# Attention and gated MLP on one core: two weight guards moved to VectorE, and new planned times for the first units

## The chip, the cores and the metric

The kernel runs on one core of a Trainium2 chip. The metric is the time of one execution on the device in microseconds (us); lower is better. Three executions of the kernel before took 531.34 to 532.36 us, median 532.01 us. The profile shown below was taken from one execution of 531.34 us, whose span, from the first to the last instruction, is 529.6 us.

## The reference

Inputs are q, k, v of shape (8, 8, 576, 64) in float32, and three weights in float64 (`w_in` 512 x 1024, `conv_w` 3 x 1024, `w_out` 1024 x 512).

```python
scores = q @ k.T / sqrt(64)                      # per batch and head
mask = (rel >= 0) & (rel < 64)                   # rel = query position - key position
attn = softmax(where(mask, scores, -1e9))        # sum + 1e-9 in the divisor
x = (attn @ v) as (batch, seq, 512)
h = relu(x @ w_in)
conv = three-tap convolution of h over seq, per channel, with conv_w
out = (h * sigmoid(conv)) @ w_out
```

## The kernel before

**Units.** The 8 x 576 = 4608 sequence positions are cut into twelve units (u = 0 to 11) of 384. For every unit the work has two halves. The attention half forms banded scores on TensorE in three blocks b (`qk`, L340), takes row maxima on VectorE (`row_max`, L353), exponentials on ScalarE (`exps`, L362), a guarded reciprocal and the division (`guard`, `reciprocal`, `normalise`, L369 to L378), a transposition (units 0 and 1: on TensorE, with a copy back by `untile` on ScalarE, L387) and four products with v (`values`, c = 0 to 3, L477). Their result is split into a high part by ScalarE (`split_hi`, L485, tile `xh`) and a remainder by VectorE (`split_lo`, L488, tile `xl`). The second half is the MLP: for each of eight chunks f, `mm1` (L501, twelve matmuls into one of two `acc` banks), `relu` (L522), then per pair of chunks i the convolution (`conv_mid` on ScalarE, `conv_side` on VectorE, L535), sigmoid, gate (L547), its split (`gate_hi`, `gate_lo`, L555), and `mm2` (L564, twelve matmuls per chunk into four `po` banks). All matmuls of the MLP work on such split pairs, three products for one.

**The banks.** The `acc` banks 0 and 1 are taken in turn by the products with v and the chunks of `mm1`. Unit 0's c = 0 to 3 take 0, 1, 0, 1, and the chunks f = 0 and 1 then 0 and 1, so `mm1` of f = 0 can't start before `split_lo` of c = 2 has read bank 0.

**The weights.** They arrive as 64-bit words and are turned into float32 on the core (`to_f32`, L244): ScalarE takes the absolute value of the high words (L248), GpSimd bounds it from below with TINY so that the exponent arithmetic can't wrap (L249, the "guard" of this document; the softmax has another one at L370), VectorE shifts and masks (L250), puts sign and exponent in (L252), ScalarE scales the low words (L255), and VectorE adds them (L256). Then GpSimd makes the high part (L269) and VectorE the remainder (L270). Chunks f = 0 and f = 1 of `w_in` are converted alone (512 elements per partition), called in0 and in1 here; then in23, in45, in67 and out01 to out67 in pairs (1024 elements). The words land in four half buffers, so that a later pair's load waits until an earlier conversion has read its half.

**The order.** Every piece of work is entered with a planned time t (the dictionary `START`, L140, and offsets to it), an engine, a cost and the tiles that it reads and writes. The pass `queued` (L61) then lays out each engine's order: it goes forward in time with the costs, and whenever an engine is free it takes, of the pieces that are ready, the one with the smallest t. The order that comes out is fixed; on the chip every engine's queue runs in it. [...] The pass also puts small matmuls on a tile of zeros (`spare`, L212) into TensorE's early gaps, up to 110 us of its own clock; they compute nothing that is used.

Of the kernel before, what the change touches and what calls it, by code (L numbers as in the profile page):

```python
# [8 lines left out]
F32 = mybir.dt.float32  # L9
# [3 lines left out]
ALU = mybir.AluOpType  # L13
# [20 lines left out]
TINY = 2.0 ** -15  # L34
# [26 lines left out]
def queued(works, fill=None):  # L61
# [30 lines left out]
    while left:  # L92
# [17 lines left out]
        if fill and e == "PE" and start < FILL_TO:  # L110
# [4 lines left out]
            if n > 0 and clean:  # L115
                order.append(Work(x.t, e, 0.0, fill(n, min(clean)[1]), [], [], None, 0, 0.0))
        turn = SWITCH[e] if e in SWITCH and (x.kind != state[e] if e == "PE" else x.kind and x.kind != state[e]) else 0.0
        if turn and e == "PE" and not x.kind:
            turn = LEAVE
        if e == "PE" or x.kind:  # L120
# [17 lines left out]


START = {  # L140
    "v0": -27.5,
    "pv0": -15.968,
    "conv": -37.437,
    "bits": ((-46.561, -47.419), (-44.383, -45.007)),
    "qk1": -43.011,
    "v1": -11.849,
    "qk2": -2.185,
    "qk0": (-91.154, -52.794, -48.024),
    "ex0": (-42.377, -37.771, -19.993),
    "sc1": (-20.012, -18.408, -14.041),  # L150
    "ex1": (-8.106, -4.046, -3.778),
    "mask": -0.529,
    "sig": ((3.087, 7.079, 8.764, 10.751), (3.178, 6.73, 5.945, 9.966), (4.046, 6.806, 8.285, 10.314)),
    "in": (-39.031, -37.38, -33.878, -12.682, -12.013),
    "out": (-11.963, -8.679, 1.926, 7.315),
# [3 lines left out]
}  # L159
SWITCH = {"PE": 0.14, "ACT": 1.28}  # L160
LEAVE = 0.24
PORT_CL = 0.5
WARM = 5.0
FILL, FILL_FROM, FILL_TO = 4.0, 2.0, 110.0

# [2 lines left out]
def attention_moe(ctx: ExitStack, tc: tile.TileContext, q, k, v, w_in, conv_w, w_out, out):  # L168
    nc = tc.nc
# [4 lines left out]
    def many(n, shape, dt, name, where=pool):  # L174
        return [where.tile(shape, dt, name=f"{name}{i}") for i in range(n)]
# [7 lines left out]
    mask = many(3, [P, P], F32, "mask")  # L183
# [13 lines left out]
    bits = [flat.bitcast(U32)[:, 4 * DM * i:4 * DM * (i + 1)].rearrange("p (e two) -> p e two", two=2) for i in range(2)]  # L197
# [20 lines left out]
    def at(t, eng, cost, do, r=(), w=(), kind=None, mb=0, port=0.0):  # L218

        plan.append(Work(t, eng, cost, do, list(r), list(w), kind, mb, port))  # L220

    def two(t, eng, cost, do, **kw):
        at(t, eng, cost, do, port=cost, **kw)
# [17 lines left out]

    def to_f32(t, n, st, x, kb, kt):  # L244

        lw, hw, xu = st[..., 0], st[..., 1], x.bitcast(U32)

        at(t, "ACT", 0.0009 * n + 0.2, lambda: nc.scalar.activation(x, hw.bitcast(F32), AF.Abs), r=kb, w=kt)  # L248
        at(t, "POOL", 0.0027 * n + 0.02, lambda: nc.gpsimd.tensor_scalar(x, x, TINY, None, op0=ALU.max), w=kt, port=PORT_CL)  # L249
        two(t, "DVE", 0.00052 * n + 0.06, lambda: nc.vector.tensor_scalar(  # L250
            xu, xu, 3, 0x3FFFFFF8, op0=ALU.logical_shift_left, op1=ALU.bitwise_and), w=kt)
        two(t, "DVE", 0.00104 * n + 0.07, lambda: nc.vector.scalar_tensor_tensor(  # L252
            xu, hw, 0xC0000000, xu, op0=ALU.bitwise_and, op1=ALU.bitwise_or), r=kb, w=kt)

        at(t, "ACT", 0.0009 * n + 0.2, lambda: nc.scalar.activation(lw, lw, AF.Copy, scale=2.0 ** -29), w=kb)  # L255
        two(t, "DVE", 0.00104 * n + 0.07, lambda: nc.vector.tensor_tensor(xu, xu, lw, ALU.add), r=kb, w=kt)  # L256

    def weights(t, src, fs, hi, lo, key, buf, halves):

        e = slice(halves[0] * DM, (halves[-1] + 1) * DM)  # L260
        st, x = bits[buf][:, e], w24[buf][:, e]
        kb, kt = [("bits", buf, a) for a in halves], [("w24", buf, a) for a in halves]
        for f, a, tl in zip(fs, halves, load_at(buf, halves, t)):
            at(tl, "SP", 0.7, lambda f=f, a=a: nc.sync.dma_start(
                bits[buf][:, a * DM:(a + 1) * DM], src[f].bitcast(U32).rearrange("p (e two) -> p e two", two=2)),
               w=[("bits", buf, a)], mb=0.52)
        n = len(fs) * DM
        to_f32(t, n, st, x, kb, kt)
        two(t, "POOL", 0.00127 * n, lambda: nc.gpsimd.tensor_copy(hi, x), r=kt, w=[f"{key}{f}h" for f in fs])  # L269
        two(t, "DVE", 0.00104 * n + 0.07, lambda: nc.vector.tensor_tensor(lo, x, hi.bitcast(F32), ALU.subtract),  # L270
           r=kt + [f"{key}{f}h" for f in fs], w=[f"{key}{f}l" for f in fs])

    freed = {}

    def load_at(buf, halves, t):

        ts = [freed.get((buf, a), START["bits"][buf][a]) for a in halves]
        for a in halves:
            freed[(buf, a)] = t + 0.01
        return ts  # L280

    def weights_in(t, fs, *where):
        f = slice(fs[0], fs[-1] + 1)
        weights(t, w_in, fs, wih[:, f].rearrange("p f c e -> p (f c e)"),
                wil[:, f].rearrange("p f c e -> p (f c e)"), "in", *where)

    def weights_out(t, fs, *where):
        f = slice(fs[0], fs[-1] + 1)
        weights(t, w_out, fs, woh[:, f].rearrange("p f e -> p (f e)"), wol[:, f].rearrange("p f e -> p (f e)"), "out", *where)

    def weights_conv(t_load, t):
        at(t_load, "SP", 0.7, lambda: nc.sync.dma_start(
            cbits, conv_w.bitcast(U32).rearrange("p (e two) -> p e two", two=2)), w=["cbits"], mb=0.03)
        to_f32(t, 3 * NF, cbits, cw.rearrange("p k f -> p (k f)"), ["cbits"], ["cw"])
# [436 lines left out]
```

## Time and profile before

| | |
|---|---|
| median of three executions | 532.01 us |
| the profiled execution | 531.34 us, span 529.6 us |
| TensorE (PE) busy | 518.5 us, 98% of the span |
| VectorE (DVE) busy | 380.3 us, 72% |
| ScalarE (ACT) busy | 379.7 us, 72% |
| GpSimd (POOL) busy | 112.6 us, 21% |
| granted TensorE clock | full over the whole span |

In rows of the profile the first column is a start or a stretch in us from the first instruction, and a busy time is the union of an engine's instructions in it. "L249" is a line of the kernel. A bracket at the end of a timeline row gives the idle time of the engine before the instruction, and what ended it. Matmuls overlap in the records: one 384-column matmul lasts 0.34 us in them, while the next starts about 0.18 us after it.

### The profile page before, as it was taken

Reading aid. Unit: us, or ns where it says so; the run is one execution under the profiler, and the core shown is the slowest. Engines: PE = TensorE matmul, PEld = TensorE weight load, DVE = VectorE, ACT = ScalarE, POOL = GpSimd, SP = SyncE. Lnnn points to the kernel's source line nnn. Section 1 sums busy time; section 2 is a strip of 40 time slices with the busy share of each in tenths; the row PEclk is TensorE's granted clock in tenths of the full one; section 3 lists DMA queues with packets and bytes.
Section 4 is the critical chain, followed back from the end, with each engine's and each line's share of the span. In section 5 each row is a group of like instructions: output and inputs, shape, how many; then the busy total and the mean of one; then the engine's idle time right before and its main releaser. Section 6 shows DMA issues by size and latency. Waiting matters only on the chain.

```text
span 529.6 us, 14836 instructions
## 1 busy us (share of the span) xinstructions
PE 518.5 (98%) x5826; PEld 499.8 (94%) x5826; DVE 380.3 (72%) x1084; ACT 379.7 (72%) x1011; POOL 112.6 (21%) x196
## 2 busy tenths in 40 slices
PE   9998999999999999999999999999999999999996
PEld 8887889999999999999999999999999999999996
DVE  3899999985858667767767767767767667655552
ACT  2997897579896696696697687687687687544542
POOL 6664467113131011021021021021021021000000
PEclk9999999999999999999999999999999999999999
DMA  8984660237292173183083074073073053010011
GB/s 284 365 296 136 208 231 1 60 109 248 76 325 72 58 256 83 42 291 77 21 297 77 16 253 122 21 285 105 13 264 120 17 152 104 16 61 0 2 60 62
DMA packets 29463, 69.98 MB, mean 132 GB/s; under 512 B 5713, under 2 KB 17617, under 8 KB 29393
## 3 DMA queue, kind: packets, MB, share of 16 engines
q1 hardware_dynamic: 29392, 69.03, 39.7%
q8 instruction: 46, 0.75, 0.6%
q14 instruction: 25, 0.20, 0.1%
HBM read 47.73 MB, written 9.47 MB: 108 GB/s over the span
## 4 chain that ended last, share of the span: by engine, by line
PE 85%; DVE 9%; DMA 1%; ACT 1%; issue 1%; SPq 1%; POOL 0%; DVEq 0%
PE po L564 39%; PE acc L501 36%; PE acc L481 6%; PE sc L350 5%; DVE c L535 1%; DVE w L252 1%; DMA T<-in_w_in_dram 1%; DVE s L357 1%; DVE w L256 1%; DVE wil L270 1%; ACT s L367 1%; SPq L234 1%; DVE xl L488 1%; DVE s L378 1%; DVE w L250 1%
## 5 line engine op out<-in xcount | busy, mean ns | idle before, releaser
L501 PE MATMUL acc<-xh,wih 128*128 128x384 f32 x384 | 131.5, 342 | 0.8 <-DVE xl L488 0.8
L564 PE MATMUL po<-gh,woh 128*128 128x386 f32 (+1 forms) x384 | 132.1, 344 | 0.0
L535 DVE SCALAR_TENSOR_TENSOR c<-hbuf,cw,c 128x386 f32<-128x386 f32 (+1 forms) x192 | 109.6, 623 | 30.7 <-ACT c L528 30.7
L564 PE MATMUL po<-gh,wol 128*128 128x386 f32 (+1 forms) x384 | 129.9, 338 | 0.0
L564 PE MATMUL po<-gl,woh 128*128 128x386 f32 (+1 forms) x384 | 129.7, 338 | 0.0
L501 PE MATMUL acc<-xh,wil 128*128 128x384 f32 x384 | 129.7, 338 | 0.0
L501 PE MATMUL acc<-xl,wih 128*128 128x384 f32 x384 | 129.7, 338 | 0.0
L367 ACT ACTIVATE s<-s,nm 128x96 f32<-128x96 f32 (+2 forms) x288 | 105.1, 367 | 5.2 <-DVE nm L357 4.9
L555 DVE TENSOR_TENSOR gl<-c,gh 128x772 fp32r<-128x772 f32 (+1 forms) x48 | 55.8, 1162 | 28.2 <-ACT gh L551 28.1
L501 PEld LDWEIGHTS acc<-xh,wih 128*128 128x128 f32 x384 | 72.1, 188 | 2.9 <-POOL sm L370 0.7
L564 PEld LDWEIGHTS po<-gh,woh 128*128 128x128 f32 x384 | 72.2, 188 | 2.6
L378 POOL TENSOR_TENSOR s<-s,r 128x768 f32<-128x768 f32 x27 | 39.7, 1472 | 163.5 <-DVE r L373 150.7
L547 DVE TENSOR_TENSOR c<-c,hbuf 128x772 f32<-128x772 f32 (+1 forms) x48 | 47.4, 987 | 36.9 <-ACT c L542 36.7
L564 PEld LDWEIGHTS po<-gl,woh 128*128 128x128 f32 x384 | 72.3, 188 | 0.0
L564 PEld LDWEIGHTS po<-gh,wol 128*128 128x128 f32 x384 | 72.3, 188 | 0.0
L501 PEld LDWEIGHTS acc<-xh,wil 128*128 128x128 f32 x384 | 72.2, 188 | 0.0
L501 PEld LDWEIGHTS acc<-xl,wih 128*128 128x128 f32 x384 | 72.1, 188 | 0.0
L522 ACT ACTIVATE hbuf<-acc 128x384 f32<-128x384 f32 x64 | 30.9, 486 | 45.8 <-PE acc L501 45.4
L542 ACT ACTIVATE c<-c 128x772 f32<-128x772 f32 (+1 forms) x48 | 40.7, 848 | 30.2 <-DVE c L535 29.9
L357 DVE CUSTOM_DVE_ANT_0 s<-sc,mask 128x96 f32<-128x96 f32 (+2 forms) x272 | 51.5, 254 | 9.7 <-POOL mask L321 5.7
L367 ACT ACTIVATION_READ_ACCUMULATOR s<-s,nm 128x1 f32 x288 | 54.3, 189 | 0.0
L511 POOL COPY hbuf<-hbuf 128x4 f32<-128x4 f32 x44 | 16.7, 379 | 176.3 <-DVE c L547 176.2
(64 smaller groups left out, 644.5 us busy)
## 6 DMA issues: line engine op xcount, KB each, us to landing
v<-in_v_dram SPq DMA_DIRECT2D x24, 768.0 KB, 7.2
ub<-T SPq DMA_DIRECT2D x240, 48.0 KB, 1.9
k<-in_k_dram SPq DMA_DIRECT2D x22, 448.0 KB, 4.9
q<-in_q_dram SPq DMA_DIRECT2D x22, 384.0 KB, 6.9
out_dram<-T SPq DMA_DIRECT2D x8, 772.0 KB, 4.2
T<-in_w_in_dram SPq DMA_DIRECT2D x8, 512.0 KB, 6.6
T<-in_w_out_dram SPq DMA_DIRECT2D x8, 512.0 KB, 4.2
out_dram<-T SPq DMA_DIRECT2D x3, 768.0 KB, 6.4
```

What stands on the lines that cost most here:

```text
L350: nc.tensor.matmul(banks_of(u, b)[h][r:r + rows, i * P + o:i * P + n], qs[hs, 2 * g + p, t:t + rows], ks[hs, 2 * g + p, t + o:t + n], star ...
L357: nc.vector.tensor_tensor_reduce(out=ss[b][:, i, h, o:n], in0=banks_of(u, b)[h][:, i * P + o:i * P + n], in1=mask[m][:, o:n], scale=-0.125 ...
L367: nc.scalar.activation(x, x, AF.Exp, bias=nms[b][:, e], scale=-1.0, accum_out=sms[b][:, e])
L378: on.tensor_tensor(sv, sv, rs[b].unsqueeze(2).broadcast_to([P, 2 * NB, n]), ALU.mult)
L481: nc.tensor.matmul(acc[bank(("v", u, c))][h * D:(h + 1) * D, t * W:(t + 1) * W], vs[:, c, t, h], ub[g][:, 2 * p:2 * p + 2, 2 * t + h], sta ...
L501: nc.tensor.matmul(acc[bank(("m", u, f))][:, :NX], w[:, f, c], x[u % 2][:, c], start=(c == 0 and j == 0), stop=(c == NC - 1 and j == 2))
L522: nc.scalar.activation(hbuf[:, f, o:o + NX], ps[:, :NX], AF.Relu)
L535: nc.vector.scalar_tensor_tensor(c, hbuf[:, f, e:e + n], cw[:, e, f:f + 1], c, op0=ALU.mult, op1=ALU.add)
L542: nc.scalar.activation(c, c, AF.Sigmoid)
L547: nc.vector.tensor_tensor(c, c, hbuf[:, 2 * i:2 * i + 2, 1:1 + n], ALU.mult)
L555: nc.vector.tensor_tensor(gls[ring(u, i)][:, :, :n], cs[i % 2][:, :, :n], ghs[ring(u, i)][:, :, :n].bitcast(F32), ALU.subtract)
L564: nc.tensor.matmul(po[o][:, :n], w[:, f, es], x, start=(f == 0 and j == 0), stop=(f == NF - 1 and j == 2))
```

## The change

Three things change. The guard of in0 and in1 (the two conversions of a single chunk) goes from GpSimd to VectorE; the pairs and `conv_w` keep theirs on GpSimd. The pass is given other costs: a GpSimd guard keeps VectorE off for 0.87 us instead of 0.5, the GpSimd copy of the high part is counted shorter, and TensorE's changes of kind a little shorter. And the planned times of units 0 to 2 are others, so that the pass writes out another order.

```diff
 START = {
-    "v0": -27.5,
-    "pv0": -15.968,
-    "conv": -37.437,
-    "bits": ((-46.561, -47.419), (-44.383, -45.007)),
-    "qk1": -43.011,
-    "v1": -11.849,
-    "qk2": -2.185,
-    "qk0": (-91.154, -52.794, -48.024),
-    "ex0": (-42.377, -37.771, -19.993),
-    "sc1": (-20.012, -18.408, -14.041),
-    "ex1": (-8.106, -4.046, -3.778),
-    "mask": -0.529,
-    "sig": ((3.087, 7.079, 8.764, 10.751), (3.178, 6.73, 5.945, 9.966), ...
-    "in": (-39.031, -37.38, -33.878, -12.682, -12.013),
-    "out": (-11.963, -8.679, 1.926, 7.315),
-    "pv": ((5.763, 4.233, 3.657, 5.767), (7.216, 7.539, 6.596, 7.589), ...
-    "ex": ((7.161, 7.971, 8.722), (9.052, 9.176, 9.461), ...
-    "qk": ((3.599, 5.779, 3.957), (7.543, 7.593, 2.551), ...
+    "v0": -33.306,
+    "pv0": -18.654,
+    "conv": -41.868,
+    "bits": ((-53.931, -59.515), (-42.565, -42.712)),
+    "qk1": -47.054,
+    "v1": -11.106,
+    "qk2": -3.441,
+    "qk0": (-91.332, -54.789, -54.623),
+    "ex0": (-38.96, -23.65, -21.941),
+    "sc1": (-18.309, -21.012, -17.336),
+    "ex1": (-8.734, -4.335, -1.498),
+    "mask": -28.064,
+    "sig": ((3.295, 7.102, 6.005, 8.503), (4.118, 5.982, 8.843, 9.99), ...
+    "in": (-44.861, -43.303, -41.22, -22.318, -18.359),
+    "out": (3.04, 3.905, 8.939, 9.322),
+    "pv": ((4.707, 4.707, 5.114, 2.178), (7.296, 7.619, 7.3, 7.626), ...
+    "ex": ((7.361, 8.28, 10.004), (7.684, 8.17, 10.173), ...
+    "qk": ((6.116, 4.695, 6.12), (3.401, 7.63, 7.634), ...
 }
-SWITCH = {"PE": 0.14, "ACT": 1.28}
-LEAVE = 0.24
-PORT_CL = 0.5
+SWITCH = {"PE": 0.12, "ACT": 1.28}
+LEAVE = 0.19
+PORT_CL = 0.87
...
-    def to_f32(t, n, st, x, kb, kt):
+    def to_f32(t, n, st, x, kb, kt, early=False):
...
-        at(t, "POOL", 0.0027 * n + 0.02, lambda: nc.gpsimd.tensor_scalar(x, x, TINY, None, op0=ALU.max), w=kt, port=PORT_CL)
+        if early:
+            two(t, "DVE", 0.00052 * n + 0.06, lambda: nc.vector.tensor_scalar(x, x, TINY, None, op0=ALU.max), w=kt)
+        else:
+            at(t, "POOL", 0.0027 * n + 0.02, lambda: nc.gpsimd.tensor_scalar(x, x, TINY, None, op0=ALU.max), w=kt, port=PORT_CL)
...
-        to_f32(t, n, st, x, kb, kt)
-        two(t, "POOL", 0.00127 * n, lambda: nc.gpsimd.tensor_copy(hi, x), r=kt, w=[f"{key}{f}h" for f in fs])
+        to_f32(t, n, st, x, kb, kt, len(fs) == 1)
+        his, los = [f"{key}{f}h" for f in fs], [f"{key}{f}l" for f in fs]
+        two(t, "POOL", 0.00104 * n, lambda: nc.gpsimd.tensor_copy(hi, x), r=kt, w=his)
```

## Rows read from the trace of the kernel before

**Rows 1.** Stretches: busy time and count by engine, granted clock, DMA share, GB/s.
```profile
0.00:38.40 38.40, 35.45 (x544) 32.60 (x544) 27.95 (x122) 27.69 (x101) 24.52 (x63) 1.00 0.88 312
38.40:60.38 21.98, 19.62 (x251) 18.03 (x251) 21.95 (x56) 17.17 (x40) 12.08 (x6) 1.00 0.45 148
60.38:70.58 10.20, 8.70 (x178) 7.78 (x177) 10.20 (x27) 9.48 (x22) 3.05 (x5) 1.00 0.85 297
70.58:75.84 5.26, 5.02 (x31) 4.70 (x28) 5.26 (x8) 5.14 (x22) 4.86 (x5) 1.00 0.71 217
75.84:526.00 450.16, 449.66 (x4829) 436.66 (x4829) 314.94 (x875) 319.98 (x829) 68.12 (x119) 1.00 0.35 111
```
**Rows 2.** The same stretches, the zero matmuls of L212 alone: PE, then weight loads.
```profile
0.00:38.40 38.40, 22.82 (x168) 21.19 (x168) 1.00 0.88 312
38.40:60.38 21.98, 0.37 (x3) 0.54 (x3) 1.00 0.45 148
60.38:70.58 10.20, 5.37 (x40) 4.66 (x40) 1.00 0.85 297
```
**Rows 3.** Stretches of VectorE alone.
```profile
19.25:76.00 56.75, 56.53 (x156) 1.00 0.69 234
```
**Rows 4.** Timeline of ScalarE: start, duration, instruction.
```profile
7.30 0.33 ACT L367 ACTIVATE s<-s,nm 128x64 f32<-128x64 f32 x1
12.29 0.67 ACT L248 ACTIVATE w<-T 128x512 f32<-128x512 f32 x1 [4.56 <-DMA T<-in_w_in_dram]
18.69 0.68 ACT L248 ACTIVATE w<-T 128x512 f32<-128x512 f32 x1
19.88 1.16 ACT L248 ACTIVATE w<-T 128x1024 f32<-128x1024 f32 x1
```
**Rows 5.** Timeline of GpSimd: the weight guards.
```profile
13.05 1.49 POOL L249 TENSOR_SCALAR w<-w 128x512 f32<-128x512 f32 x1 [2.97 <-ACT w L248]
19.50 4.58 POOL L249 TENSOR_SCALAR w<-w 128x512 f32<-128x512 f32 x2
32.28 2.78 POOL L249 TENSOR_SCALAR w<-w 128x1024 f32<-128x1024 f32 x1
```
**Rows 6.** Timeline of VectorE.
```profile
14.57 0.43 DVE L250 TENSOR_SCALAR w<-w 128x512 uint32<-128x512 uint32 x1 [2.14 <-POOL w L249]
15.03 0.69 DVE L252 SCALAR_TENSOR_TENSOR w<-T,w 128x512 uint32<-128x512 uint32 x1
21.49 1.41 DVE L252 SCALAR_TENSOR_TENSOR w<-T,w 128x512 uint32<-128x512 uint32 x1
22.82 1.21 DVE L378 TENSOR_TENSOR s<-s,r 128x1024 f32<-128x1024 f32 x1
30.20 1.21 DVE L378 TENSOR_TENSOR s<-s,r 128x1024 f32<-128x1024 f32 x1
32.35 2.05 DVE L270 TENSOR_TENSOR wil<-w,wih 128x1024 fp32r<-128x1024 f32 x1
37.74 0.55 DVE L488 TENSOR_TENSOR xl<-acc,xh 128x384 fp32r<-128x384 f32 x1
40.66 1.21 DVE L256 CUSTOM_DVE_ANT_0 w<-T,w 128x2048 uint16<-128x2048 uint16 x1
47.35 1.22 DVE L270 TENSOR_TENSOR wil<-w,wih 128x1024 fp32r<-128x1024 f32 x1
65.68 0.68 DVE L250 TENSOR_SCALAR w<-w 128x1024 uint32<-128x1024 uint32 x1
66.28 1.79 DVE L555 TENSOR_TENSOR gl<-c,gh 128x772 fp32r<-128x772 f32 x1
68.00 1.21 DVE L252 SCALAR_TENSOR_TENSOR w<-T,w 128x1024 uint32<-128x1024 uint32 x1
71.12 1.22 DVE L270 TENSOR_TENSOR wol<-w,woh 128x1024 fp32r<-128x1024 f32 x1
```
**Rows 7.** Timeline of TensorE.
```profile
38.44 0.41 PE L501 MATMUL acc<-xh,wih 128*128 128x384 f32 x1 [0.56 <-DVE xl L488]
```

More of the change, by code (lines that the diff above doesn't have):

```diff
@@ L140 @@
 START = {
-    "v0": -27.5,
-    "pv0": -15.968,
-    "conv": -37.437,
-    "bits": ((-46.561, -47.419), (-44.383, -45.007)),
-    "qk1": -43.011,
-    "v1": -11.849,
-    "qk2": -2.185,
-    "qk0": (-91.154, -52.794, -48.024),
-    "ex0": (-42.377, -37.771, -19.993),
-    "sc1": (-20.012, -18.408, -14.041),
-    "ex1": (-8.106, -4.046, -3.778),
-    "mask": -0.529,
-    "sig": ((3.087, 7.079, 8.764, 10.751), (3.178, 6.73, 5.945, 9.966), (4.046, 6.806, 8.285, 10.314)),
-    "in": (-39.031, -37.38, -33.878, -12.682, -12.013),
-    "out": (-11.963, -8.679, 1.926, 7.315),
[3 rows of a table removed]
-}
-SWITCH = {"PE": 0.14, "ACT": 1.28}
-LEAVE = 0.24
-PORT_CL = 0.5
+    "v0": -33.306,
[10 more added lines that the diff above has]
+    "mask": -28.064,
+    "sig": ((3.295, 7.102, 6.005, 8.503), (4.118, 5.982, 8.843, 9.99), (4.046, 6.806, 8.285, 10.314)),
+    "in": (-44.861, -43.303, -41.22, -22.318, -18.359),
+    "out": (3.04, 3.905, 8.939, 9.322),
[3 rows of a table added]
+}
+SWITCH = {"PE": 0.12, "ACT": 1.28}
+LEAVE = 0.19
+PORT_CL = 0.87
 WARM = 5.0
@@ L267, in weights @@
         n = len(fs) * DM
-        to_f32(t, n, st, x, kb, kt)
-        two(t, "POOL", 0.00127 * n, lambda: nc.gpsimd.tensor_copy(hi, x), r=kt, w=[f"{key}{f}h" for f in fs])
-        two(t, "DVE", 0.00104 * n + 0.07, lambda: nc.vector.tensor_tensor(lo, x, hi.bitcast(F32), ALU.subtract),
-           r=kt + [f"{key}{f}h" for f in fs], w=[f"{key}{f}l" for f in fs])
+        to_f32(t, n, st, x, kb, kt, len(fs) == 1)
+        his, los = [f"{key}{f}h" for f in fs], [f"{key}{f}l" for f in fs]
+        two(t, "POOL", 0.00104 * n, lambda: nc.gpsimd.tensor_copy(hi, x), r=kt, w=his)
+        two(t, "DVE", 0.00104 * n + 0.07, lambda: nc.vector.tensor_tensor(lo, x, hi.bitcast(F32), ALU.subtract), r=kt + his, w=los)
     freed = {}
```

6 rows, old and new, of the table START are left out of this document.

## The prediction

> **What bounds the kernel.** I first read the stretches, then the zero matmuls inside them, then VectorE's own stretch, then the timelines. From 75.84 to 526.00 us TensorE is busy 449.66 of 450.16 us [rows 1]: from there on it goes without a gap, and the change touches nothing of that work. Ahead of 75.84 it is different. TensorE is busy 35.45 + 19.62 + 8.70 + 5.02 = 68.79 us there, so it is idle 7.05 us; of the busy time, 22.82 + 0.37 + 5.37 = 28.56 us are zero matmuls [rows 2]. Lost in all: 35.6 us, in three places. Before the first `mm1` it is 38.40 - 35.45 + 22.82 = 25.8; from there to 60.38 it is 2.7; from 60.38 to 70.58 it is 1.50 + 5.37 = 6.9. Only this loss can change. What paces the ramp is VectorE: from 19.25 to 76.00 it is busy 56.53 of 56.75 us [rows 3]. So a gain is VectorE time saved or filled ahead of 76 us, or VectorE work put in an order that frees more TensorE work early. The clock is full in every stretch, so nothing comes from it. The profiled execution took 531.34 us (span 529.6 and 1.7 around it), 0.67 below the median; I sum on 531.34 and add 0.67 at the end.
>
> **The guard of in0.** ScalarE delivers at 12.29 + 0.67 = 12.96, having waited 4.56 us for the load [rows 4]. The GpSimd guard runs from 13.05 for 1.49, and VectorE, idle for 2.14 us, starts L250 at 14.57 [rows 5, 6]. On VectorE the guard has the shape and kind of L250, 0.43 us [rows 6]: from about 13.0 to 13.4, so L250 starts near 13.4, 1.2 earlier. Bounds: 1.5 if VectorE's start after ScalarE costs nothing, 0 if the load lands later. The chain is the only work VectorE has there, so I take -1.2. An early wait on ScalarE for that load stays: the exponentials behind it (those at 7.30 were the last before it) wait too.
>
> **The guard of in1.** The two GpSimd guards from 19.50 (in1, in23) take 4.58 together, and L252 of in1 takes 1.41 beside them against 0.69 alone [rows 5, 6]: 0.72 lost on a VectorE that has no idle time. The new guard costs it 0.43. Net -0.3; bounds -0.7 (it falls into a gap) and +0.4 (another instruction meets in23's guard instead). GpSimd is relieved of about 1.5, and in23's guard can start up to that much sooner.
>
> The trace says what such a meeting costs. L270 of in23 takes 2.05 beside the guard at 32.28, the same instruction 1.22 at 47.35 [rows 5, 6], and 0.83 is the usual size; yet the division at 22.82 takes 1.21 within the 19.50 pair, as the one at 30.20 does. [...]
>
> **The costs of the pass.** They issue nothing; they change the order only. 0.87 is near the 0.83 just read, where 0.5 was not, so the pass will be less surprised by a held-up VectorE. Between 21 and 76 us I count seven instructions stretched by 0.7 to 0.9, the first at 21.49, the last the 1.79 at 66.28 [rows 6]. The bounds are all others of them gone (six times 0.83, 5.0 us) and one more (+0.8); nothing says that many go, since the guards of the pairs still run beside a full VectorE. I take one: -0.8.
>
> **The order.** Working the pass by hand from the planned times, four things move.
> - in0, in1 and in23 (-44.9, -43.3, -41.2) now go ahead of block 0's exponentials (-39.0), which preceded in0 before. in1's absolute value (0.68 at 18.69 [rows 4]) falls ahead of most of block 0's exponentials on ScalarE, and its VectorE steps fall into the stretch before 19.25, where VectorE had room. Block 0's division waits for it: to 2 us later, hidden as long as VectorE has other work.
> - The load of in23's first half falls behind the four q and k loads of unit 1 on the DMA queue. Its ScalarE step, at 19.88 [rows 4], was not waiting for a load; it becomes the late one only if the load slips past 20 us. I cost it at nothing; if that cover is gone, in23 slips, and VectorE has unit 1's maxima to do.
> - in45 (-12.7 to -22.3) goes ahead of unit 0's `split_lo` (-16 to -18.7). Its L256, 1.21 at 40.66, ran after c = 2's `split_lo` at 37.74 and can now run before it; that `split_lo` is what the first `mm1` at 38.44 waits for [rows 6, 7]. So the first `mm1` does not gain all that VectorE gains: +1.2 on this place, given back when in45 and in67 are needed.
> - out01 and out23 (-12.0, -8.7 to 3.0, 3.9) go behind unit 1's softmax and the first convolution. Two steps of out23 (0.68 at 65.68, 1.21 at 68.00) stood ahead of out01's L270 at 71.12 [rows 6]: up to 1.9 that can give way to what feeds TensorE sooner. But out01 itself is planned later, and `mm2` can't start without it.
>
> With the guards of in23, in45 and in67 asked for sooner (2.78 each on GpSimd [rows 5]), VectorE gets gaps that it did not have: working by hand I find some 2 to 3 us of them around 33 and 40 us. Against that stands the room before 19.25, filled. For the order as a whole the bounds are -5.4 (the loss from 60.38 to 70.58 less 1.5, that is nearly all of it) and +3.1 (L256 and L270 of in45 and in1's 0.68 ahead of the first `mm1`: 1.21 + 1.22 + 0.68). I take +0.4: half of out23's 1.9 gained, 1.3 of gaps lost. It is the weakest term.
>
> **Sum.** -1.2 - 0.3 - 0.8 + 0.4 = -1.9: 531.34 - 1.9 = 529.4 for the profiled execution, 530.1 as a median.
>
> **Rivals.**
> 1. *The middle gap closes.* From 60.38 to 70.58 TensorE does 8.70 - 5.37 = 3.3 us of useful work [rows 1, 2]. If in67 and the last chunks of `mm1` are ready there (two chunks, twelve matmuls each at about 0.18: 4.2 us), the loss falls by 4.2 on top of a small gain of 0.3: 531.34 - 4.5 = 526.8, median 527.5. For it: in67 is planned 6 earlier, and out weights stop preceding unit 1's work. Against: VectorE is full there, and ScalarE is busy 9.48 of 10.20 us.
> 2. *The gain is given back.* VectorE runs earlier by 1.5, but out01's chain, planned 15 later, sets the start of `mm2`, and TensorE waits at the end of the ramp instead of at its start. Or the change does not do what it says: in0 still waits for its load, which no guard makes earlier. 531.3, median 532.0. For it: the 4.56 us wait is a load's.
> 3. *The first `mm1` comes later: slower.* Weights before softmax puts 1.21 + 1.22 + 0.68 = 3.1 us of weight work ahead of c = 2's `split_lo`, against 1.5 gained by the guards: +1.6, 532.9, median 533.6. It decides if the first `mm1` starts after 40.0 and the loss behind it is no smaller. Against: that work has to be done at some time, and in45 done is TensorE work free later.
>
> **How the numbers follow.** About 0.2% (1.1 us) is what a measurement can tell from no change. The forecast, 0.42 (with 528.3 to 531.4 as its own range); the middle gap closing, 0.17; given back, 0.19; slower, 0.22. Of the forecast's share about 0.04 lies within 1.1 us. Faster: 0.38 + 0.17 = 0.55; same: 0.04 + 0.19 = 0.23; slower 0.22. The range runs from just under rival 1 to rival 3: 526.9 to 533.6.
>
> **What would show it.** Right: L250 of in0 starts near 13.4 with no GpSimd instruction before it; VectorE from 13 to 19 nearly full; zero matmuls and idle time of TensorE ahead of its last gap at 33 to 34 us in sum instead of 35.6. The first `mm1` near 38. Wrong: a first `mm1` after 40, new gaps of VectorE beyond 3 us between 30 and 45, or a start of `mm2` later than before by more than `mm1` is ahead. If the last gap of TensorE is followed by others beyond 80 us, my reading of the ramp as the only place is wrong.

## The result, and the profile after

The changed kernel takes 534.02 us (median of five runs, 533.45 to 534.10), the kernel before 532.01 on the same chip: 1.0036 times as long, 95% interval 1.0025 to 1.0048. That is slower by 0.36%, where 530.1 and faster was forecast, and above the stated range of 526.9 to 533.6. The profiled execution took 534.02 us (span 532.2), 2.7 more than the one of before.

In the code after, three lines further down from L253 on: the new guard on VectorE is L250, GpSimd's L252, `mm1` L504, `mm2` L567, `gate_lo` L558, the products with v L484, `split_lo` L491.

The first view answers to [rows 1]: stretches with PE, PEld, DVE, ACT and POOL busy, granted clock, DMA share, GB/s.
```profile
0.00:41.44 41.44, 38.26 (x563) 35.68 (x563) 30.30 (x128) 29.81 (x106) 21.80 (x60) 1.00 0.84 294
41.44:64.80 23.36, 21.20 (x258) 20.01 (x254) 22.01 (x44) 18.59 (x39) 9.71 (x7) 1.00 0.50 155
64.80:76.00 11.20, 11.19 (x140) 10.45 (x140) 11.20 (x36) 8.01 (x15) 10.98 (x12) 1.00 0.71 246
76.00:526.00 450.00, 449.73 (x4876) 433.95 (x4875) 320.78 (x880) 326.20 (x856) 62.82 (x118) 1.00 0.36 112
```
The same stretches, the tile of zeros alone (PE, PEld, DVE), as in [rows 2]:
```profile
0.00:41.44 41.44, 25.76 (x186) 24.04 (x186) 0.17 (x1) 1.00 0.84 294
41.44:64.80 23.36, 4.41 (x34) 4.08 (x34) 0.00 (x0) 1.00 0.50 155
```
TensorE loses 41.44 - 38.26 + 25.76 = 28.9 us ahead of the first `mm1` and 23.36 - 21.20 + 4.41 = 6.6 up to 64.80, in all 35.5, against 35.6 before. In this execution the ramp (the time up to 76 us) has moved its loss forward and gained next to nothing. VectorE alone, against the 56.53 us of [rows 3]:
```profile
19.25:76.00 56.75, 53.16 (x147) 1.00 0.66 220
```

The time is lost after the ramp. To see where, I follow one row that every unit has, the 48 products with v, in unit 4 and in unit 11.
```profile
176.34 1.62 PE L484 MATMUL acc<-ub,v 128*64 128x64 f32 x48
460.56 1.62 PE L484 MATMUL acc<-ub,v 128*64 128x64 f32 x48
```
Before, the same rows:
```profile
176.64 1.62 PE L481 MATMUL acc<-ub,v 128*64 128x64 f32 x48
458.56 1.62 PE L481 MATMUL acc<-ub,v 128*64 128x64 f32 x48
```
At 176 us the changed kernel is 0.3 ahead, which is nothing: the four kernels e1, e5, e6 and e7 below, whose ramp has the same order, have this row at 175.96 to 177.21. At 460 it is 2.0 behind. The seven units between take 284.22 instead of 281.92: 0.33 more each. (The last 0.6 of the 2.6 in span lies behind the issue of the last output transfer: 528.02 to 532.2 against 525.98 to 529.6.) The chain of waits names the place. After (start, us, what):
```profile
199.03 2.15 DVE gl L558
201.23 2.04 PE po L567 x10
...
238.32 3.16 PE acc L504 x18
241.83 2.04 PE po L567 x10
243.88 1.05 PE acc L504 x6
244.93 2.12 PE po L567 x12
...
282.42 2.00 PE po L567 x10
```
Before:
```profile
238.25 4.23 PE acc L501 x24
242.47 4.24 PE po L564 x24
```
Before, 24 matmuls of the next unit's `mm1` are followed by 24 of `mm2`. After, six of the `mm1` stand behind the first twelve of `mm2`, and two of these twelve are missing from the chain's piece: they ran, and the third waited. The timelines of TensorE and VectorE there:
```profile
241.14 0.34 PE L504 MATMUL acc<-xl,wih 128*128 128x384 f32 x1
241.32 0.34 PE L567 MATMUL po<-gh,woh 128*128 128x386 f32 x1
241.49 0.34 PE L567 MATMUL po<-gh,wol 128*128 128x386 f32 x1
241.83 0.44 PE L567 MATMUL po<-gl,woh 128*128 128x386 f32 x1
242.11 0.34 PE L567 MATMUL po<-gh,woh 128*128 128x386 f32 x1
...
239.66 2.12 DVE L558 TENSOR_TENSOR gl<-c,gh 128x772 fp32r<-128x772 f32 x1 [0.32 <-ACT gh L554]
```
`gate_lo` ends at 241.78. The matmul that reads `gl` starts at 241.83 instead of 241.49 + 0.18 = 241.67: 0.16 late. It then lasts 0.44, and the next starts 0.28 later, not 0.18: another 0.10. That is 0.26 of the 0.33 per unit. The two more changes between `mm1` and `mm2` that the new order has cost nothing there: the six matmuls at 243.88 take 1.05 in the chain and the twelve at 244.93 take 2.12, the usual 0.18 each. No row puts an idle bracket there, because the records of the matmuls overlap (241.49 + 0.34 is 241.83); it shows in the chain and in the spacing. `gate_lo` itself is as early as before (239.64 there, 2.12 long); TensorE has come to it 1.0 us earlier, six matmuls at 0.18.

### The profile page after: what moved, and what is told of

Its sections match the earlier page's. It is cut to its first block, busy times and chain, and to the rows that moved or that the text cites. A ratio compares the mean times of both kernels' runs of the same rounds, so it can differ in the third digit from the quotient of the medians.

```text
span 532.2 us, 14856 instructions
## 1 busy us (share of the span) xinstructions
PE 521.9 (98%) x5836; PEld 501.3 (94%) x5836; DVE 385.2 (72%) x1086; ACT 383.9 (72%) x1015; POOL 105.3 (20%) x194
## 4 chain that ended last, share of the span: by engine, by line
PE 76%; ACT 10%; DMA 5%; DVE 4%; SPq 2%; POOL 1%; issue 1%; ACTq 0%
PE po L567 34%; PE acc L504 30%; PE acc L484 6%; PE sc L353 4%; ACT s L370 3%; SPq L420 2%; DMA v<-in_v_dram 2%; DVE gl L558 2%; DMA T<-in_w_in_dram 2%; PE acc L212 1%; DMA T<-in_w_out_dram 1%; POOL w L252 1%; ACT L545 1%; ACT L370 1%; ACT c L531 1%; ACT hbuf L525 1%
## 5 line engine op out<-in xcount | busy, mean ns | idle before, releaser
L504 PE MATMUL acc<-xh,wih 128*128 128x384 f32 x384 | 131.5, 343 | 2.1 <-ACT hbuf L525 2.1
L567 PE MATMUL po<-gh,woh 128*128 128x386 f32 (+1 forms) x384 | 132.4, 345 | 0.0
L567 PE MATMUL po<-gl,woh 128*128 128x386 f32 (+1 forms) x384 | 130.5, 340 | 0.3
L567 PE MATMUL po<-gh,wol 128*128 128x386 f32 (+1 forms) x384 | 130.0, 338 | 0.0
L504 PE MATMUL acc<-xh,wil 128*128 128x384 f32 x384 | 129.8, 338 | 0.0
L504 PE MATMUL acc<-xl,wih 128*128 128x384 f32 x384 | 129.6, 338 | 0.0
L504 PEld LDWEIGHTS acc<-xh,wih 128*128 128x128 f32 x384 | 72.1, 188 | 4.3 <-ACT hbuf L525 2.3
L567 PEld LDWEIGHTS po<-gh,woh 128*128 128x128 f32 x384 | 72.2, 188 | 2.8
L567 PEld LDWEIGHTS po<-gl,woh 128*128 128x128 f32 x384 | 72.3, 188 | 2.5 <-DVE gl L558 2.5
L550 DVE TENSOR_TENSOR c<-c,hbuf 128x772 f32<-128x772 f32 (+1 forms) x48 | 51.6, 1075 | 29.9 <-ACT c L545 29.6
L567 PEld LDWEIGHTS po<-gh,wol 128*128 128x128 f32 x384 | 72.3, 188 | 0.1
L504 PEld LDWEIGHTS acc<-xh,wil 128*128 128x128 f32 x384 | 72.2, 188 | 0.0
L504 PEld LDWEIGHTS acc<-xl,wih 128*128 128x128 f32 x384 | 72.2, 188 | 0.0
L558 DVE TENSOR_TENSOR gl<-c,gh 128x772 fp32r<-128x772 f32 (+1 forms) x48 | 56.3, 1176 | 16.1 <-ACT gh L554 15.5
L531 ACT ACTIVATE c<-hbuf,cw 128x386 f32<-128x386 f32 (+1 forms) x96 | 53.5, 608 | 1.1 <-DVE gl L558 1.1
```

Source lines behind the costliest of these rows:

```text
L504: nc.tensor.matmul(acc[bank(("m", u, f))][:, :NX], w[:, f, c], x[u % 2][:, c], start=(c == 0 and j == 0), stop=(c == NC - 1 and j == 2))
L531: nc.scalar.activation(cs[i % 2][:, a, :n], hbuf[:, f, 1:1 + n], AF.Copy, scale=cw[:, 1, f:f + 1])
L550: nc.vector.tensor_tensor(c, c, hbuf[:, 2 * i:2 * i + 2, 1:1 + n], ALU.mult)
L558: nc.vector.tensor_tensor(gls[ring(u, i)][:, :, :n], cs[i % 2][:, :, :n], ghs[ring(u, i)][:, :, :n].bitcast(F32), ALU.subtract)
L567: nc.tensor.matmul(po[o][:, :n], w[:, f, es], x, start=(f == 0 and j == 0), stop=(f == NF - 1 and j == 2))
```

## The experiments

The first theory: the loss is the order of the later units, which the pass writes differently because of `SWITCH` and `LEAVE`. Rivals: the guards on VectorE, or a worse ramp. The first four kernels tell these apart. "Marks" are the two rows above in a kernel's own profile. The kernel before was measured again beside each group of runs, at 531.49 to 531.87; ratios are to that.

**e1**: after, with the old costs in the pass from unit 3 on.
```diff
         if turn and e == "PE" and not x.kind:
             turn = LEAVE
+        if turn and e == "PE" and start > 130:
+            turn = 0.14 if x.kind else 0.24
```


> The kernel after, with one edit: from 130 us of the ordering pass's own clock on, TensorE's changes of kind cost 0.14 and 0.24 in it again, so that units 3 to 10 get the order of the kernel before while the order of the ramp stays that of the kernel after. Theory A (the loss sits in the later units: 0.3 us in each of about eight): 534.0 - 2.4 = 531.6 us, unit period 40.3 instead of 40.6. Theory B (the loss sits in the ramp, the first mm1 at 41.4 instead of 38.4): 534.0, no change.

Measured: 531.16, ratio 0.9993 (0.9984 to 1.0002). Marks 177.21 and 459.06: 281.85 apart, as before.

**e2**: before, with the new costs there.
```diff
+        if turn and e == "PE" and start > 130:
+            turn = 0.12 if x.kind else 0.19
```


> The kernel before, with one edit: from 130 us of the ordering pass's own clock on, TensorE's changes of kind cost 0.12 and 0.19, so that the later units get the order of the kernel after behind the ramp of the kernel before. Theory A: 532.0 + 2.4 = 534.4, period 40.6. Theory B: 532.0, period 40.3.

Measured: 534.46, ratio 1.0054 (1.0041 to 1.0067). Marks 284.14 apart. So two numbers of the pass make the whole loss, without any other part of the change; and what is left of the change (e1) is worth -0.07%, which can't be told from nothing.

**e3**: e1, with the guards of in0 and in1 run by GpSimd at the same places in the order.
```diff
-            two(t, "DVE", 0.00052 * n + 0.06, lambda: nc.vector.tensor_scalar(x, x, TINY, None, op0=ALU.max), w=kt)
+            two(t, "DVE", 0.00052 * n + 0.06, lambda: nc.gpsimd.tensor_scalar(x, x, TINY, None, op0=ALU.max), w=kt)
```


> The first kernel of this set with the guards of in0 and in1 given to GpSimd at the same places of the same order (the pass still plans them as VectorE's). If the guard's move is worth what the prediction gave it (1.2 + 0.3), this is 1.5 slower than the first kernel, 533.1. If other waits of the ramp take it back, it is within 0.3 of it, 531.6.

Measured: 531.21, ratio 0.9997 (0.9982 to 1.0012): as e1.

**e4**: before, with these two guards on VectorE and the order kept.
```diff
-        at(t, "POOL", 0.0027 * n + 0.02, lambda: nc.gpsimd.tensor_scalar(...
+        at(t, "POOL", 0.0027 * n + 0.02, lambda: (nc.vector if n == DM else nc.gpsimd).tensor_scalar(...
```


> The kernel before with the guards of in0 and in1 run by VectorE at the same places of the same order, nothing else changed. By the prediction's terms: L250 of in0 at 13.4 instead of 14.57 and 1.5 less, 530.5. If the fixed order behind it takes the gain back: 532.0. If the 0.43 added twice to a full VectorE decides: 532.4 to 532.9.

Measured: 531.83, ratio 1.0000 (0.9990 to 1.0009). From both sides the move of the guards is worth nothing.

Two differences of TensorE's order remain in the later units: half of `mm1` f = 0 behind `mm2` f = 2, and `mm2` f = 0, bank 1, ahead of a half of `mm1` f = 5. Each was undone by itself in the list that the pass returns.

**e5**: the half `mm1` put back ahead of `mm2` f = 2.
```diff
...
+            if order.index(z) < order.index(y) < order.index(x):
+                order.remove(x)
+                order.insert(order.index(y), x)
...
```


> The kernel after; in the order that the pass has written, the second half of the next unit's mm1 f = 0 is put back ahead of mm2 f = 2 wherever the pass had put it behind (units 3 to 9). If the wait for gl behind the first half is the 0.3 us of each unit, this gives 534.0 - 2.1 = 531.9 and the TensorE wait at some 21 us into each unit is gone. If the other swap, or VectorE's and ScalarE's order, is the cause, 534.0.

**e6**: the other one put back; **e7**: both.
```diff
...
+            if order.index(x) < order.index(y):
+                order.remove(x)
+                order.insert(order.index(y) + 1, x)
...
```


> The kernel after; only the other swap of TensorE is undone: mm2 f = 0 of bank 1 is put back behind mm1 f = 5 in units 2 to 10. It should do nothing (534.0) if the first swap is the cause, and give 531.9 if this one is.

> Both swaps of TensorE undone, VectorE and ScalarE in the order of the kernel after. If TensorE's order alone is the cause: 531.2 to 531.9, like the run with the old costs of change from 130 us on. If VectorE's and ScalarE's order has a part: between that and 534.0.

Measured: e5 531.48 (0.9993, 0.9983 to 1.0003), marks 282.02 apart; e6 533.47 (1.0028, 1.0018 to 1.0039), 284.23 apart; e7 530.90 (0.9986, 0.9976 to 0.9997), 281.93 apart. One swap is the whole loss, the other is nothing. In e5 the same place reads
```profile
242.20 0.34 PE L567 MATMUL po<-gh,woh 128*128 128x386 f32 x1
242.38 0.34 PE L567 MATMUL po<-gh,wol 128*128 128x386 f32 x1
242.56 0.36 PE L567 MATMUL po<-gl,woh 128*128 128x386 f32 x1
```
with 0.18 between all of them: `gl` was done at 241.6 (239.47 + 2.12) and nobody waited.

The ramp was the second question: its first `mm1` comes 3.0 later than before (and up to 5.1 in e5, at 43.50, with the same order of the ramp), as rival 3 said, and yet its loss is the same. After, ScalarE's and TensorE's rows from 45 us on:
```profile
47.87 1.15 ACT L248 ACTIVATE w<-T 128x1024 f32<-128x1024 f32 x1 [2.55 <-DMA T<-in_w_out_dram]
48.92 1.12 ACT L258 ACTIVATE T<-T 128x1024 uint32<-128x1024 uint32 x1
49.94 0.47 ACT L525 ACTIVATE hbuf<-acc 128x384 f32<-128x384 f32 x1
...
51.85 0.44 PE L504 MATMUL acc<-xh,wih 128*128 128x384 f32 x1 [2.08 <-ACT hbuf L525]
```
out01's absolute value stands in ScalarE's queue and waits 2.55 us for its load; the `relu` behind it is what TensorE waits 2.08 for.

**e8**: e1, with that absolute value behind the first `conv_mid`; **e10**: e7 with the same.
```diff
...
+        x = next(x for x in order if x.eng == "ACT" and x.t == START["out"][0])
+        y = next(x for x in order if x.eng == "ACT" and abs(x.t - 1.4) < 1e-6)
...
+        order.remove(x)
+        order.insert(order.index(y) + 1, x)
...
```


> The kernel after with the old costs of change from 130 us on, and one step moved in the written order: ScalarE's absolute value of out01, which held its queue for 2.55 us at 45.3 to 47.9 in wait of a load, goes behind the first conv_mid. If that wait is what holds the relu that TensorE waits 2.08 us for at 51.85, the ramp is 1 to 2 us shorter: 529.2 to 530.2. If the acc banks and the attention of unit 1 hold TensorE at 57 to 65 anyway: 531.2, no change.

> The kernel after with both swaps of TensorE undone in the later units (VectorE and ScalarE there in the order of the kernel after) and out01's step later on ScalarE. If the two edits add up: 530.9 - 0.6 = 530.3. It tells whether ScalarE's and VectorE's new order of the later units costs anything by itself: against 530.6 with the old one.

Measured: e8 530.56 (0.9980, 0.9970 to 0.9989), e10 531.08 (0.9980, 0.9970 to 0.9991). TensorE's wait at 51.85 is gone. Against e1's 0.9993 the gain is 0.13% by e8, some 0.7 us, against e7's 0.9986 it is 0.06% by e10. The intervals of each pair overlap, so one pair alone doesn't show it. All the kernels do: those with this move and no load or zero matmul misplaced (e8, e10 and, below, e13 to e15) have ratios of 0.9976 to 0.9980 and the first mark at 174.41 to 175.49; those without it (e1, e3, e5 and e7) 0.9986 to 0.9997 and 176.05 to 177.21. It is less than the 2.08 of the row; that wait is not the same in every execution, 0.21 in e5 with the same order of the ramp.

**e9**, **e13**, **e14** and **e15** put softmax work ahead of the weights again in e8: c = 1's and c = 2's `split_lo` ahead of in45's L253 and L259 (VectorE), and a block of unit 1's scores behind the products that feed the first `mm1`, and one of unit 2's behind that `mm1` itself (TensorE). e13 has both, e14 the first alone, e15 the second alone. e9 was meant to be e13, but a zero matmul carries the planned time of what follows it, and in e9 it was the zero matmuls that moved: 14 of them, 1.71 us, in between the first two chunks of `mm1`. The lines are e15's; e9 and e13 have the last one without its last condition.
```diff
...
+        ahead(step("DVE", pv + 0.7), step("DVE", START["in"][3]))
+        behind(step("PE", START["sc1"][2]), step("PE", pv + 1.0))
+        behind(step("DVE", START["in"][3], 2), step("DVE", pv + 1.2))
+        behind(step("PE", START["qk"][0][1]), next(x for x in order if x.eng == "PE" and abs(x.t - 0.01) < 1e-6 and x.w))
...
```


> The run before with out01's step later, and in the ramp unit 0's attention put ahead of what the new planned times had put before it: on VectorE split_lo of c = 1 ahead of in45's L253, and split_lo of c = 2 ahead of in45's L259; on TensorE the scores of unit 1's block 2 behind the products of c = 2, and those of unit 2's block 1 behind the first mm1. The first mm1 should start 1.5 to 2.5 us earlier. If the late first mm1 is what took the ramp's gain (the prediction's third rival), the time falls by as much: 528.5 to 529.0. If VectorE's sum of work sets the end of the ramp, whatever TensorE does first: 530.6, and the gap moves to 50 to 65 us.

> The move of the run before, now with the scores themselves (that run had moved the zero matmuls ahead of them): on VectorE split_lo of c = 1 ahead of in45's L253 and split_lo of c = 2 ahead of in45's L259; on TensorE unit 1's block 2 scores behind the products of c = 2, unit 2's block 1 scores behind the first mm1. The first mm1 starts 1.5 to 2.5 us earlier. If the late first mm1 took the ramp's gain: 530.6 - 1.5 to 2.0 = 528.6 to 529.1. If it does not set the end of the ramp: 530.6 within 0.5, with the loss moved behind the first mm1.

> Of that move the VectorE part alone. If VectorE's order holds the first mm1: 1 us less than 530.6. If the scores ahead of it on TensorE hold it: 530.6, no change.

> Of that move the TensorE part alone. If the scores ahead of it hold the first mm1: 1 us less than 530.6. If split_lo on VectorE holds it: 530.6; if unit 1's maxima come later for it and in67 with them: 531 to 531.5.

Measured: e9 533.35 (1.0021, 1.0012 to 1.0031); e13 530.36 (0.9976, 0.9966 to 0.9987); e14 530.28 (0.9977, 0.9968 to 0.9986); e15 530.23 (0.9979, 0.9970 to 0.9987). The first `mm1` is at 39.70 in e13 against 42.64 in e8, 2.9 earlier, and the first mark at 175.37 against 175.49: 0.1. Apart from e9's, these ratios can't be told from e8's 0.9980. An early start of `mm1` isn't what ends the ramp. In e9 the zero matmuls in the wrong place cost what they last: its first mark is 177.21, 1.72 after e8's.

**e11**: e8, with in23's first load ahead of unit 1's q and k.
```diff
...
+        x = next(x for x in order if x.eng == "SP" and x.t == START["bits"][1][0])
+        y = next(x for x in order if x.eng == "SP" and x.t == START["qk1"])
+        order.remove(x)
+        order.insert(order.index(y), x)
...
```


> The run with out01's step later, and the load of in23's first half put back ahead of unit 1's q and k on the DMA queue. In the kernel after ScalarE waited 0.70 us for it at 20.6. If that wait is on the ramp's path: 0.4 to 0.7 less, 530.0. If not: 530.6; if unit 1's scores then come late: 531.

Measured: 531.31 (0.9992, 0.9983 to 1.0000): the gain of e8 is gone again, and the first mark is 0.7 later (176.21). The intervals still overlap a little (0.9983 to 0.9989); what is clear is that this load ahead gains nothing.

**e16**, **e17**, **e18**: if not the start, do the zero matmuls behind it hold TensorE? They are written in fixed numbers and run even when real work is ready. e16 is e13, e17 is before, without those after 45 us of the pass's clock; e18 is e13 without those after 30.
```diff
-FILL, FILL_FROM, FILL_TO = 4.0, 2.0, 110.0
+FILL, FILL_FROM, FILL_TO = 4.0, 2.0, 45.0
```


> The kernel that had the softmax splits ahead of in45's steps, out01 later and the old costs from unit 3 on (530.36), without the zero matmuls that it writes after 45 us of the plan: its trace has some 4.4 us of them between 45 and 76 us (6 at 54.77, 10 at 59.37, 18 at 61.41), with almost no idle time beside them. Theory A: they hold TensorE while real work is already ready behind them, so that they set the ramp's end: 1 to 3 us less, 527.4 to 529.4, and the products with v at 176 us move earlier by as much. Theory B: the real work is not ready any sooner; idle time stands where the zero matmuls stood, and the time is 530.4 within 0.4. Rival C: with TensorE idle there the granted clock falls to its lower level in a stretch, and the kernel gets slower than 531.

> The kernel before without the zero matmuls written after 45 us of the plan (some 5.7 us in its trace from 38.40 to 76 us, 2.93 of them in one row at 66.14). A: 1 to 3 us less, 529.0 to 531.0. B: 532.0 within 0.4, with idle time in their place. C: a lower granted clock and more than 532.5.

> The first kernel of this call with the zero matmuls stopped at 30 us of the plan already, so that the stretch from 30 to 41 us, where they fill the time ahead of the first mm1, has none either. A: a further gain only if real work was ready behind them there; from the rows, where the first mm1 waits for VectorE's split, I expect none: as the first within 0.4. [...]

Measured: e16 531.02 (0.9986, 0.9976 to 0.9996), e17 533.47 (1.0030, 1.0019 to 1.0040), e18 531.07 (0.9993, 0.9984 to 1.0003). Theory A falls: no gain in any of the three, and e17 is clearly slower. e13, then e16, at the same `mm1`:
```profile
54.77 0.92 PE L214 MATMUL po<-spare 128*128 128x112 f32 x6
57.18 0.42 PE L506 MATMUL acc<-xh,wih 128*128 128x384 f32 x1 [1.49 <-DVE xl L493]
57.44 0.34 PE L506 MATMUL acc<-xh,wil 128*128 128x384 f32 x1
```
```profile
56.73 0.66 PE L506 MATMUL acc<-xh,wih 128*128 128x384 f32 x1 [2.33 <-DVE xl L493]
57.19 0.52 PE L506 MATMUL acc<-xh,wil 128*128 128x384 f32 x1
57.51 0.52 PE L506 MATMUL acc<-xl,wih 128*128 128x384 f32 x1
```
Both wait for VectorE's `split_lo`; the zero matmuls only fill the wait. Without them the matmuls that follow are spaced by 0.32 instead of 0.18. The granted clock is lower there (0.57 in e16 from 56.00 to 60.00), and e17's stretches (all columns) show it plainly:
```profile
60.00:64.80 4.80, 2.94 (x52) 2.29 (x51) 4.80 (x22) 3.85 (x6) 1.67 (x4) 0.89 0.96 289
64.80:74.00 9.20, 5.63 (x96) 5.20 (x97) 9.20 (x11) 8.09 (x27) 3.58 (x6) 0.50 0.68 229
74.00:80.00 6.00, 6.00 (x36) 6.00 (x35) 5.40 (x8) 4.83 (x20) 4.14 (x2) 1.00 0.67 246
```
The granted clock is 0.50 from 64.80 to 74.00, after TensorE had idled for some 1.9 of 4.8 us, and e17 is 1.8 us longer than the kernel before. By these rows what ends the ramp is the later `split_lo`s and what they wait for, spread over VectorE, ScalarE and GpSimd. No run shows it, and which single piece would shorten it stays open.

## Why the prediction was wrong

**The step that failed** is in its first part: "from there on it goes without a gap, and the change touches nothing of that work". The count of busy time is right, the second half is not: `SWITCH` and `LEAVE` are costs of the pass for every unit. "They issue nothing; they change the order only" was said of the costs, and `PORT_CL` alone was followed up. In units 3 to 9 0.02 and 0.05 us less in the plan were enough for `mm2` f = 2 to go ahead of a half `mm1`, 0.33 us each time, 2.3 us in all (e1, e2, e5). A TensorE that is full before has no slack against an order that is worse, so [rows 1] should have been read as a warning. The last line of the prediction named this as what would refute it; the delay made no idle row, though, and was to be found only by the period of the units and the chain. The ramp's -1.9 failed as well: e1, which has the ramp of the change without the later units, is at 0.9993, not to be told from no change. Its terms follow.

**The guards, -1.5 forecast, 0 measured** (e3, e4). The first step did what was said: in0's shift L253 starts 0.4 after the guard, at 13.77 where near 13.4 was forecast, with no GpSimd before it. What failed is "the chain is the only work VectorE has there". After, ScalarE first, then VectorE ([rows 4 to 6] answer):
```profile
12.21 1.25 ACT L248 ACTIVATE w<-T 128x512 f32<-128x512 f32 x2 [3.31 <-DMA T<-in_w_in_dram]
14.90 0.68 ACT L258 ACTIVATE T<-T 128x512 uint32<-128x512 uint32 x1
16.26 0.67 ACT L258 ACTIVATE T<-T 128x512 uint32<-128x512 uint32 x1
...
13.32 0.42 DVE L250 TENSOR_SCALAR w<-w 128x512 f32<-128x512 f32 x1
13.77 0.43 DVE L253 TENSOR_SCALAR w<-w 128x512 uint32<-128x512 uint32 x1
16.95 0.69 DVE L259 CUSTOM_DVE_ANT_0 w<-T,w 128x1024 uint16<-128x1024 uint16 x1 [0.15 <-ACT T L258]
18.15 1.07 DVE L274 TENSOR_TENSOR wil<-w,wih 128x512 fp32r<-128x512 f32 x1 [0.50 <-POOL wih L273]
```
The chain has more branches, which I left out: ScalarE's scale of the low words (L258), which stands behind exponentials in its queue and which in1's add waits for at 16.95, and GpSimd's high part, which the remainder L274 waits 0.50 for. In e3, with GpSimd's guards, the remainder L276 of in0 starts at 18.14, after at 18.15. e4 shows the same in the order of before:
```profile
14.02 0.43 DVE L250 TENSOR_SCALAR w<-w 128x512 uint32<-128x512 uint32 x1
16.20 0.20 DVE L373 RECIPROCAL r<-sm 128x8 f32<-128x8 f32 x1 [1.02 <-POOL sm L370]
17.58 0.68 DVE L256 CUSTOM_DVE_ANT_0 w<-T,w 128x1024 uint16<-128x1024 uint16 x1
```
The shift L250 starts 0.55 earlier than in [rows 6], although the load came 0.56 later (L248 at 12.85); then VectorE's queue has the reciprocal and the division of a softmax block ahead of the add L256, and the reciprocal waits 1.02 for the softmax guard. The add starts at 17.58, where before it was 17.25: the gain went into that wait, of which the late load is a part, since the exponentials stand behind L248 on ScalarE.

**The costs of the pass, -0.8 forecast for one meeting fewer.** More went: where the prediction counted seven stretched instructions, the last at 66.28, the new order has three up to 72 us (31.73 and 42.88, 1.50 and 1.51 against 0.69 at 25.23, and the pair at 51.21, 1.93 against 1.14 at 55.63); behind them each order has one more, at 73.39 before and 72.95 after. VectorE's busy time from 19.25 to 76 fell by 3.4 us (56.53 to 53.16). A part of this is work that went ahead of 19.25, where VectorE is busy 10.36 us instead of 8.99; up to 76 it is 2.0 less in all. That bought nothing: VectorE got 3.6 us of gaps. So "what paces the ramp is VectorE" was too simple; a full engine in the profile was partly full of instructions stretched beside GpSimd's (its copies L273 start at 31.66, 42.81 and 51.37), and the waits of the ramp run through all four engines.

**The order, +0.4 forecast.** Loss of the ramp 35.5 against the 33 to 34 forecast. The first `mm1` came at 41.44, as rival 3 had it, with in45's add L259 at 39.00 ahead of the `split_lo` at 40.14 (and, which it didn't have, a block of scores ahead of `mm1` on TensorE); but the loss behind it fell from 9.8 to 6.6, so that rival's price (+1.6) was not paid, and e13 shows that its place decides nothing. The time came out near rival 3's (533.6) by another mechanism, which is luck. "A gain given back" (rival 2) fits e1 by its number alone: what it gave as the cause, a late start of `mm2`, didn't come. The first `mm2` of after, then of before:
```profile
67.99 0.44 PE L567 MATMUL po<-gh,woh 128*128 128x386 f32 x1
72.80 0.34 PE L564 MATMUL po<-gh,woh 128*128 128x386 f32 x1
```
It starts 4.8 earlier, and the ramp is no shorter for it. The load of in23 did slip (ScalarE waits 0.70 for it at 20.59), but costing it at nothing is right: e11 gains nothing by putting it first. out01's load on ScalarE, some 0.7 us (e8), was not seen.

## What to carry to other kernels

A parameter of an ordering pass touches all that the pass orders, so compare the order of every stage, above all of the stage where an engine is full: there every swap that comes to its operand earlier than the producer is paid once per unit. Measure a repeated loss by one row per unit, not by idle time; 0.3 us in each of seven units is in no list of gaps. And before an engine's earlier step is credited, follow every input of the next step, also those that stand behind other work in a queue.

The best versions here are e8, e10 and e13 to e15, 0.20 to 0.24% below the kernel before and not to be told apart: the change with TensorE's old order in the later units and with out01 later.

## What was not expected of the hardware

- After, TensorE waited 0.16 us for an operand at 241.83 and lost 0.26: the first matmul behind the wait lasted 0.44 instead of 0.34 and the next followed after 0.28 instead of 0.18.
- Not every VectorE instruction beside a GpSimd guard was stretched. In e3 the two guards span 12.29 to 15.24; the two-input L257 at 14.68 took 0.69 beside them, as at 15.74 behind them, where before L252, of the same shape, took 1.41 beside the guards from 19.50 [rows 5, 6], while the one-input shift L255 at 13.82 took 0.83, against 0.42 at 15.29.
- GpSimd's guards of the pairs are not always 2.78 us long as in [rows 5]: after, 3.37, 3.19 and 3.15 at 21.83, 28.51 and 39.70. The new planned cost didn't bring this, since before has one of 3.75 at 50.77.
